# Linear attention and two feed-forward layers on one core: queries of blocks 1 to 8 loaded by halves of a head's components and turned by VectorE

## The chip, the cores and the metric

The kernel runs on one core of one Trainium2 chip. The metric is the device time of one execution in microseconds (us). The time before is 1531.42 us, the median of three runs (1531.21 to 1534.8).

## The reference, cut to what matters

```python
# q, k, v: [8, 8, 576, 64] (batch, head, sequence, component); all inputs float32 in the reference
kv  = einsum('bhsd,bhse->bhde', k, v)
out = einsum('bhsd,bhde->bhse', q, kv)
rms = sqrt(mean(out * out, axis=-1) + 1e-06)
x   = (out / rms * g_norm)              # to [4608 tokens, 512]
h   = x @ w_in1                         # 512 x 2048
x   = (max(h, 0) + alpha * min(h, 0)) @ w_out1
h   = x @ w_in2
out = (h * sigmoid(1.702 * h)) @ w_out2
```

The kernel reads the weights as 64-bit words and turns them into 32-bit values itself.

## The kernel before

The 4608 tokens are nine blocks (0 to 8) of 512 tokens. Layer 0 of block 0, 1 and 2 and layer 1 of block 0 run as plain products (`plain`): a step m is one 128-wide piece of the 2048 inner columns, made by `gemm_in` (12 matmuls of 128x512, bank h) and, two steps later, `gemm_out` (12 matmuls, bank y). All other blocks run two at a time through `pairs`, with seven products in place of eight (banks X, Z, V, W). Every value and weight is split into a high and a low part (`note_split`: ScalarE writes the high part, VectorE the rest), and a product is three matmuls; all of them are issued at L937.

The program has three stretches. The start reads keys, values and queries, and makes block 0's input. The plain stretch follows, in 48 steps: block 0 up to piece MH - 1, block 1 whole, the rest of block 0, block 2. The pairs and the last plain block take the remainder. Along the plain stretch the kernel also does the attention of blocks 1 to 8 (the jobs below), turns the sixteen weight pieces of layer 0 (`weight`, `weight1`), and begins their sums (`weights1`), which the pairs read back from memory.

A job is a piece of attention work put between two half-steps of the plain stretch; `JOBS` gives each block its first half-step and the number of half-steps over which its jobs are spread. Job k (`job_kv`) makes keys times values. Job q (`job_q`) prepares queries for two heads, p = 0 to 3 for the block's eight heads. Job o (`job_out`) multiplies queries by keys-times-values on TensorE (tile ops), and ScalarE and VectorE do the norm (L583 mean of squares, L599 scaling). Job x (`job_x`) hands the result on: for blocks 2 to 8 VectorE transposes 32x32 squares (L638) and SyncE stores it (L645).

Job q before: the block's queries are loaded by SyncE with tokens on the partitions (L523, runs of 64 components, 256 bytes). For each p, TensorE transposes four 128x128 squares into PSUM (L545, tile qTps), and ScalarE copies the bank to SBUF (L553, tile qT). For blocks 1 to 8 that is 128 transposes and 32 copies.

The order of the work is not written out by hand. Every operation is noted with its engine, its estimated cost and its dependences (`note`); `arrange` then plays these against one another and gives each operation a place in its engine's queue and a place in SBUF; `emit` writes the queues in that order. Each engine takes its queue strictly in order. All DMAs are issued from SyncE's queue. SBUF places are shared by many tiles, so a name such as dr__477 or kvb in a row is that of the place's first tenant, not of the value.

Of the kernel before, what the change touches and what calls it, by code (L numbers as in the profile page):

```python
# [10 lines left out]
F32 = mybir.dt.float32  # L11
# [8 lines left out]
P = 128  # L20
# [4 lines left out]
MH = 6  # L25
# [25 lines left out]
ACT2, DVE2, POOL2 = 1.06, 1.17, 2.35  # L51
KB1, B256, B512 = 1.1, 1.77, 1.3

HOP_ASIDE = 0.8
AHEAD = {"wt": 10.0, "xs": 20.0, "xc": 80.0, "gr": 8.0, "ld": 14.0, "raw": 45.0, "w2p": 12.0, "x": 15.0}
SLACK = 10.0
SPARE = {"8": 3, "4": 3, "2": 3}
SPARE_W = {"8": 1, "4": 2, "2": 3}

BACKLOG = 2.0  # L60
URGENT = 10.0
LD_LOW = {"4": 10}
ADDS = 4
PASSES = 12
SEED = 153
GAP, SLOW = 1.8, 3.4

RINGS = (3, 2, 2, 6)
# [11 lines left out]
def linear_attention_two_ffn_kernel(  # L80
# [52 lines left out]
    xd = {j: dram.tile([KC, P, TB], F32, name=f"xd{j}") for j in range(min(2, PLAIN), NB)}  # L133
# [23 lines left out]
    pe_clock = [0.0]  # L157

    def note(eng, cost, fn, reads=(), writes=(), new=(), ahead=None, slack=SLACK, low=None, mb=0.0, two=False, aside=False, calm=False):
# [6 lines left out]
        o.aside, o.calm = aside, calm  # L166
# [5 lines left out]
        for key in reads:  # L172
            if key in last_write:
                o.deps.add(last_write[key])
            readers.setdefault(key, []).append(o)
# [12 lines left out]
        ops.append(o)  # L188

# [22 lines left out]
    def arrange(before, ahead, urgent, spread):  # L212
# [6 lines left out]
        for o in ops:  # L219

            if o.eng == "PE":
                o.late = before[o.n] if before else o.clock
                now_ = o.late + o.cost
                o.base = o.late
            else:
                o.late = now_ + o.slack if o.slack is not None else 1e9
            o.land = o.cost + (LAND + o.mb / RATE if o.eng == "SP" else 0.0)
        for o in reversed(ops):
            late = [a.late - spread * (HOP if a.eng != o.eng else 0.0) - o.land for a in after[o.n]]
            o.late = min([o.late] + late)  # L230
        unit = [0.0] * (UNITS + 8)
# [69 lines left out]
        def arrive(o):  # L301
# [4 lines left out]
            if o.ahead is not None and line and o.late - ahead * o.ahead > line[0].late:  # L306
                held.append((o.late - ahead * o.ahead, o.n, o))
# [20 lines left out]
        def choose(e, spare, dma_at):  # L328
# [3 lines left out]
            for o in ready[e]:  # L332
# [7 lines left out]
                if o.need:  # L340
                    r = room_at(o, spare and o.late > t + urgent)
# [10 lines left out]
        for _ in range(len(ops)):  # L352
# [15 lines left out]
            if line and o is line[0]:  # L368
                line.popleft()
# [10 lines left out]
            if o.two or o.eng == "POOL":  # L380
                other = "POOL" if o.two else "DVE"
                cost += max(0.0, port[other] - t)
# [33 lines left out]
    def emit():  # L416
        found = (1e9, None)
        rng = random.Random(SEED)
        for i in range(PASSES):
            options = (1.0, URGENT, 1.0) if i < 2 else (rng.uniform(0.7, 1.3), rng.uniform(0.0, 30.0), rng.uniform(0.5, 4.0))  # L420
            got = arrange(found[1] if i else None, *options)
# [24 lines left out]

    def load_kv(b, p):
# [13 lines left out]

        note("SP", 2 * ISSUE, load, writes=[(key, 0)], new=[(key, [P, 2 * TB], F32, "4")], ahead=AHEAD["ld"], slack=None, mb=0.52 * KB1, low=LD_LOW if b > 1 else None)
        if p == 0:
            note("SP", 2 * ISSUE, load_rest, writes=[(("kR",), 0), (("vR",), 0)], ahead=AHEAD["ld"], slack=None, mb=0.26 * B256)

# [15 lines left out]
    def job_kv(b, p):  # L481
# [13 lines left out]

        for i in pp:
            load_kv(b, i)
# [11 lines left out]
    def job_q(j, p):  # L509

        bank, qT = ("qTps", j, p), ("qT", j, p)
        src = ("ldq", j, p if j == 0 else 0)

        def load0():
# [6 lines left out]
        def load(t):  # L521
            for off, n, b, s in runs((NT4 * j + t) * P, P):
                nc.sync.dma_start(  # L523
                    out=tl(src)[off : off + n, t * TB : (t + 1) * TB].rearrange("p (h d) -> p h d", h=H),
                    in_=q[b, :, s : s + n, :].rearrange("h p d -> p h d"),
                )

        if j == 0:
            note(
# [876 lines left out]
```

## Time and profile before

| | |
|---|---|
| median of three runs | 1531.42 us |
| profiled execution, whole time | 1531.49 us |
| profiled execution, span from first to last instruction | 1529.6 us |
| TensorE matmul, busy | 1504.7 us (98%), 7376 matmul instructions recorded |
| TensorE weight load, busy | 1244.8 us (81%) |
| VectorE, busy | 1119.4 us (73%) |
| ScalarE, busy | 760.4 us (50%) |
| GpSimd, busy | 329.8 us (22%) |
| hardware DMA queue, share of 16 engines | 78.9% |
| mean granted TensorE clock | 0.997 |

The whole time of the profiled execution is 1.9 us above its span. Shares are means over stretches that differ much, so the profile is to be read by stretch: first where TensorE stands idle, then what the removed instructions take from its stream, then how full VectorE and the DMA engines are where the added work goes.

### The profile page before, as it was taken

What the parts mean: (1) busy time and instruction counts of PE and PEld (TensorE: products, weight loads), DVE (VectorE), ACT (ScalarE), POOL (GpSimd) and SP (SyncE); (2) the same over time, 40 slices, a digit from 0 to 9 for tenths busy, and PEclk for the clock granted to TensorE, in tenths of its full rate; (3) what the DMA queues carried; (4) which work ended last, traced back from release to release, by engine and by line L of the source; (5) the groups of instructions that cost most, each with busy time, mean ns of one, the idle gap of its engine ahead of it and who ended that gap; (6) DMA issues with size and microseconds to landing.
All of it is one profiled execution on the core that took longest, in us unless ns stands there. A gap on an engine that the chain in (4) does not pass through costs nothing.

```text
span 1529.6 us, 19788 instructions
## 1 busy us (share of the span) xinstructions
PE 1504.7 (98%) x7376; PEld 1244.8 (81%) x7376; DVE 1119.4 (73%) x1148; ACT 760.4 (50%) x971; POOL 329.8 (22%) x282
## 2 busy tenths in 40 slices
PE   5999999999999999999999999999999999999998
PEld 4788888888788888888888888888888888888886
DVE  4899965698979998999899668654855485547511
ACT  4876544545555455554555555444634463444221
POOL 2444540685231134123424220000000000000000
PEclk9999999999999999999999999999999999999999
DMA  9998785858989799989998987676767676756962
GB/s 274 323 325 255 209 237 140 247 177 268 340 278 327 234 346 327 331 288 350 332 322 279 356 314 237 207 236 205 238 208 235 205 237 208 234 193 205 286 195 83
DMA packets 240495, 393.49 MB, mean 257 GB/s; under 512 B 93968, under 2 KB 124688, under 8 KB 240400
## 3 DMA queue, kind: packets, MB, share of 16 engines
q1 hardware_dynamic: 240400, 392.23, 78.9%
q8 instruction: 59, 0.97, 0.3%
q14 instruction: 36, 0.29, 0.1%
HBM read 302.00 MB, written 90.18 MB: 256 GB/s over the span
## 4 chain that ended last, share of the span: by engine, by line
PE 96%; DVE 1%; DMA 1%; ACT 1%; issue 1%; POOL 0%; SPq 0%; DVEq 0%; ACTq 0%; POOLq 0%
PE V L937 20%; PE X L937 19%; PE W L937 15%; PE Z L937 15%; PE y L937 11%; PE h L937 11%; PE ops L568 2%; PE kvps L477 1%; PE qTps L545 1%; DMA ldkv<-in_v_dram 1%; POOL ldkv L784 0%; SPq L453 0%; DVE gl L1184 0%; PE xTps L660 0%; POOL kvb L784 0%
## 5 line engine op out<-in xcount | busy, mean ns | idle before, releaser
L937 PE MATMUL V<-gr,pi 128*128 128x512 f32 x852 | 215.7, 389 | 0.5 <-DVE gr L706 0.5
L937 PE MATMUL X<-xc,gs 128*128 128x512 f32 x840 | 213.0, 389 | 0.1
L937 PEld LDWEIGHTS V<-gr,pi 128*128 128x128 f32 x852 | 159.8, 188 | 34.0 <-DVE gr L706 0.9
L937 PEld LDWEIGHTS X<-xc,gs 128*128 128x128 f32 x840 | 157.6, 188 | 33.2 <-DVE gl L1184 0.5
L937 PE MATMUL Z<-xc,gs 128*128 128x512 f32 x660 | 166.8, 389 | 0.0
L937 PE MATMUL W<-gr,pi 128*128 128x512 f32 x636 | 161.1, 389 | 0.0
L937 PEld LDWEIGHTS Z<-xc,gs 128*128 128x128 f32 x660 | 123.9, 188 | 25.7
L937 PE MATMUL h<-x,w 128*128 128x512 f32 x546 | 140.5, 398 | 3.5 <-DVE x L672 3.4
L937 PEld LDWEIGHTS W<-gr,pi 128*128 128x128 f32 x636 | 119.4, 188 | 24.8
L937 PE MATMUL X<-xc,pi 128*128 128x512 f32 x492 | 124.3, 389 | 0.0
L937 PE MATMUL V<-gr,gs 128*128 128x512 f32 x480 | 121.5, 389 | 0.0
L937 PEld LDWEIGHTS h<-x,w 128*128 128x128 f32 x546 | 101.3, 190 | 24.3 <-DVE x L672 4.0
L937 PE MATMUL y<-gs,w 128*128 128x512 f32 x480 | 118.8, 395 | 0.9 <-DVE gs L706 0.9
L706 DVE TENSOR_TENSOR gr<-gt,gr 128x1024 fp32r<-128x1024 f32 x84 | 103.6, 1239 | 17.8 <-ACT gr L699 17.7
L1182 DVE TENSOR_TENSOR gt<-Z,gt 128x512 f32<-128x512 f32 x64 | 44.0, 688 | 97.4 <-PE Z L937 92.8
L937 PEld LDWEIGHTS X<-xc,pi 128*128 128x128 f32 x492 | 92.3, 188 | 19.4 <-ACT gl L1192 0.3
L699 ACT ACTIVATE gr<-gt 128x1024 fp32r<-128x1024 f32 x84 | 87.9, 1054 | 36.2 <-DVE gt L901 14.3
L937 PEld LDWEIGHTS V<-gr,gs 128*128 128x128 f32 x480 | 90.1, 188 | 18.7
L937 PEld LDWEIGHTS y<-gs,w 128*128 128x128 f32 x480 | 88.3, 188 | 19.3 <-DVE gs L706 1.2
L706 DVE TENSOR_TENSOR gr<-gl,gr 128x1024 fp32r<-128x1024 f32 x56 | 73.3, 1309 | 31.9 <-ACT gr L699 31.9
L937 PE MATMUL W<-gr,gs 128*128 128x512 f32 x372 | 93.6, 389 | 0.0
L937 PE MATMUL Z<-xc,pi 128*128 128x512 f32 x348 | 88.0, 389 | 0.0
(515 smaller groups left out, 2554.5 us busy)
## 6 DMA issues: line engine op xcount, KB each, us to landing
gs<-w1wi SPq DMA_DIRECT2D x68, 512.0 KB, 4.8
pi<-w0wo SPq DMA_DIRECT2D x63, 512.0 KB, 5.0
pi<-w1wo SPq DMA_DIRECT2D x63, 512.0 KB, 3.7
gs<-w0wi SPq DMA_DIRECT2D x60, 512.0 KB, 5.5
pi<-w1wi SPq DMA_DIRECT2D x53, 512.0 KB, 4.7
gs<-w1wo SPq DMA_DIRECT2D x51, 512.0 KB, 3.7
raw<-in_moe_w_in_dram SPq DMA_DIRECT2D x16, 1024.0 KB, 7.6
raw<-in_moe_w_out_dram SPq DMA_DIRECT2D x16, 1024.0 KB, 7.8
```

The lines of the kernel that those rows point to most:

```text
L477: nc.tensor.matmul(tl(("kvps", b))[sl, p, sl], lhsT=lhsT, rhs=rhs, start=(r == 0), stop=(r == R), skip_group_check=True)
L545: nc.tensor.transpose(tl(bank)[:, t * P : (t + 1) * P], tl(src)[:, x : x + P], ident)
L568: nc.tensor.matmul((tl(("ops", j, heads[i])) if j else tl(bank)[:, i])[off : off + n, t], lhsT=tl(("qT", j, heads[i]))[:, t * P + off : t ...
L699: "ACT", ACT2 if both else ACT, lambda: nc.scalar.activation(out=part(0), in_=value(), func=AF.Copy, scale=1.0 if scale is None else scale),
L706: nc.vector.tensor_tensor(out=part(1), in0=value(), in1=high, op=ALU.subtract)
L937: nc.tensor.matmul(o, lhsT=x, rhs=y, start=start and n == 0, stop=stop and n == 2, skip_group_check=True)
L1182: nc.vector.tensor_tensor(out=val(), in0=tl(bank), in1=val(), op=ALU.add)
```

## The change

For blocks 1 to 8 the queries are loaded in another layout, so that 32x32 transposes alone turn them. One load (tile ldq) holds four heads (two values of p). Its partitions are four groups of 32: head h of a pair (0 or 1) and half a of its 64 components. Within a group lie 32 tokens on the partitions and 32 components in a run (128 bytes). VectorE's stream transpose of the whole 128x1024 tile swaps tokens and components within each 32x32 square, which gives qT for two p at once. TensorE's 128 transposes and ScalarE's 32 copies for these blocks are gone; block 0 keeps its own.

A load is issued per group of 32 partitions, and per p, or per run of 32 tokens where the block crosses from one batch entry into the next with fewer than 128 tokens. SyncE issues 240 such DMAs in the program where it issued 36 before; the piece of the most common form in block 1 is 32x14x32 (57 KB), the smallest 32x2x32 (8 KB).

The diff also changes the planner's numbers (`AHEAD`, `SPARE`, a table `SHIFT` of due times), and with them the order on every engine. MH goes from 6 to 8, so that block 0 runs eight pieces before block 1 starts. The jobs of blocks 3 to 8 are spread over later half-steps. In `weights1` one GpSimd addition of 128x1024 becomes four of 128x256, sixteen times. HALF = 8 and KEPT = 8 equal the number of pairs of pieces, so the branches on them are not taken, and no other work is added.

```diff
-MH = 6
+MH = 8
...
-J1 = (2, 8)
+J1 = (1, 9)
...
-JOBS = {2: (13, 11), 3: (24, 11), 4: (35, 11), 5: (46, 11), 6: (57, 11), 7: (68, 11), 8: (79, 11)}
+JOBS = {2: (12, 11), 3: (28, 10), 4: (39, 11), 5: (51, 12), 6: (71, 8), 7: (79, 9), 8: (88, 7)}
...
-RINGS = (3, 2, 2, 6)
+RINGS = (3, 1, 2, 7)
...
     def job_q(j, p):
+        if j:
+            return job_q_turned(j, p // 2) if p % 2 == 0 else None
...
+    def job_q_turned(j, pp):
+        src, qT = ("ldq", j, pp), ("qT", j, pp)
+        todo = []
+        for off, n, b, s in runs(TB * j, TB):
+            u = off // 32
+            if n // 32 < 4:
+                todo += [(u + x, None, b, s + 32 * x, n) for x in range(n // 32)]
+            else:
+                todo += [(u, p, b, s, n) for p in range(2)]
+        def load(i):
+            h, a = i // 2, i % 2 * 32
+            to = tl(src)[32 * i : 32 * (i + 1)].rearrange("x (p n f) -> x p n f", p=2, f=32)
+            for u, p, b, s, n in todo:
+                if p is None:
+                    nc.sync.dma_start(
+                        out=to[:, :, u],
+                        in_=q[b, 4 * pp : 4 * pp + 4, s : s + 32, a : a + 32].rearrange("(p h) x f -> h x p f", h=2)[h],
+                    )
+                else:
+                    nc.sync.dma_start(
+                        out=to[:, p, u : u + n // 32],
+                        in_=q[b, 4 * pp + 2 * p + h, s : s + n, a : a + 32].rearrange("(n x) f -> x n f", x=32),
+                    )
+        for i in range(4):
+            note(
+                "SP", 0.4 * len(todo), lambda i=i: load(i), reads=[(src, 0)] if i else [], writes=[(src, i)],
...
+        note(
+            "DVE", DVE2, lambda: nc.vector.transpose(tl(qT), tl(src)),
+            reads=[(src, i) for i in range(4)], writes=[(qT, 0), held_by[qT]],
+            new=[(qT, [P, 2 * TB], F32, "4")], low={"4": 2},
+        )
...
                 def whole(da=da, w=w):
                     t = tl(w).bitcast(F32).rearrange("p e h i f -> p (e h) i f")
-                    nc.gpsimd.tensor_tensor(
-                        out=tl(da).rearrange("p (n f) -> p n f", n=4), in0=t[:, :, 0], in1=t[:, :, 1], op=ALU.add
-                    )
+                    for n in range(4):
+                        nc.gpsimd.tensor_tensor(
+                            out=tl(da)[:, n * HB : (n + 1) * HB], in0=t[:, n, 0], in1=t[:, n, 1], op=ALU.add
+                        )
```

The queues below are those of the place where block 1's queries come in, while block 0's first pieces run. Line numbers of the changed kernel differ: matmuls stand at L1035 (L937 before), the attention product at L647 (L568), the weight conversion at L850, L852 and L865 (L761, L763 and L776), the low parts at L793 and L795 (L706 and L708), the first layer's activation at L999 (L901), the new loads at L606 and L611, and the stream transpose of queries at L624.

TensorE before, from the fourth piece of block 0 (h) to block 1's first attention products (ops):

```order
L937 MATMUL h<-x,w 128x512 x6
L545 MATMUL qTps<-ident,ldq 128x128 x8
L937 MATMUL h<-x,w 128x512 x3
L545 MATMUL qTps<-ident,ldq 128x128 x8
L937 MATMUL h<-x,w 128x512 x3
L937 MATMUL y<-gs,w 128x512 x3
L568 MATMUL ops<-kvb,da 64x128 x2
```

TensorE in the changed kernel, from the fourth piece (h) to the same products:

```order
L1035 MATMUL h<-x,w 128x512 x12
L1035 MATMUL y<-gs,w 128x512 x12
L1035 MATMUL h<-x,w 128x512 x12
L647 MATMUL ops<-kvb,dr__487 64x128 x2
```

The sixteen transposes are gone, and the products of block 1 stand 21 matmuls of 512 columns later in the stream than before.

VectorE in the changed kernel, at that place (gs is the low part that y's matmuls read, w a weight's low part, xn a weight in conversion):

```order
L793 TENSOR_TENSOR gs<-ldkv,gs 128x512
L850 TENSOR_SCALAR xn<-xn 128x1024
L852 TENSOR_SCALAR xn<-xn 128x1024
L624 STREAM_TRANSPOSE dr__487<-kvb 128x1024
L793 TENSOR_TENSOR w<-dr__487,w 128x4x256
L624 STREAM_TRANSPOSE dr__487<-ldkv 128x1024
L865 SCALAR_TENSOR_TENSOR xn<-raw,xn 128x512 x2
L999 SCALAR_TENSOR_TENSOR ldkv<-ldkv,alpha_sb 128x512
```

Two stream transposes have come into VectorE's queue; a weight's low part stands between them, and a weight conversion and the next activation behind them.

SyncE's queue before, where block 1's queries are loaded (raw is a weight piece of 1 MB):

```order
L460 DMA kR<-in_k_dram 64x8x64
L460 DMA kR<-in_v_dram 64x8x64
L523 DMA ldq<-in_q_dram 64x8x64 x2
L728 DMA raw<-in_moe_w_in_dram 128x4x256
L733 DMA raw<-in_moe_w_out_dram 128x2x512 x2
L523 DMA ldq<-in_q_dram 128x8x64 x3
L728 DMA raw<-in_moe_w_in_dram 128x4x256
```

SyncE's queue in the changed kernel, from the sixth weight piece on (eight of the 32 query pieces stand earlier, before and behind the third weight piece):

```order
L817 DMA raw<-in_moe_w_in_dram 128x4x256
L822 DMA raw<-in_moe_w_out_dram 128x2x512 x2
L606 DMA kvb<-in_q_dram 32x2x32 x2
L611 DMA kvb<-in_q_dram 32x14x32 x2
L606 DMA kvb<-in_q_dram 32x2x32 x2
L611 DMA kvb<-in_q_dram 32x14x32 x2
L606 DMA kvb<-in_q_dram 32x2x32 x2
L611 DMA kvb<-in_q_dram 32x14x32 x2
L606 DMA ldkv<-in_q_dram 32x2x32 x2
```

Twenty-four small query pieces now stand behind the eighth weight piece, where five larger ones stood between the third and the seventh.

## Rows read from the trace of the kernel before

**Rows 1.** Windows: stretch, busy per engine, granted clock, DMA share, GB/s.

```profile
core 0: us, PE busy (x) PEld busy (x) DVE busy (x) ACT busy (x) POOL busy (x), PEclk, DMA share, GB/s
0.00:62.00 62.00, 43.91 (x347) 34.71 (x348) 39.24 (x54) 38.17 (x57) 21.92 (x30) 0.94 1.03 289
62.00:210.00 148.00, 148.00 (x1020) 123.91 (x1020) 133.13 (x161) 96.94 (x139) 69.63 (x62) 1.00 0.85 259
210.00:375.00 165.00, 164.23 (x951) 136.41 (x950) 122.65 (x137) 80.70 (x119) 74.71 (x57) 1.00 0.72 213
375.00:1437.00 1062.00, 1061.48 (x4681) 878.02 (x4680) 809.30 (x777) 523.61 (x622) 163.49 (x135) 1.00 0.80 269
1437.00:1530.00 93.00, 87.04 (x385) 71.73 (x383) 15.05 (x22) 20.97 (x36) 0.00 (x0) 0.99 0.53 170
```

**Rows 2.** TensorE's waits: line, who released it, us in total, times, longest.

```profile
PE kvps L477 <- DMA kvb<-in_v_dram: 4.4, 1, 4.4
PE h L937 <- DVE x L672: 3.4, 1, 3.4
PE ops L568 <- ACT kvb L553: 2.3, 1, 2.3
PE xTps L660 <- DVE xn L599: 1.9, 1, 1.9
```

**Rows 3.** TensorE's timeline: start, us, line, form, count, idle before.

```profile
52.05 0.94 PE L937 MATMUL h<-x,w 128*128 128x512 f32 x3
52.83 1.04 PE L545 MATMUL qTps<-ident,ldq 128*128 128x128 f32 x8
53.62 0.94 PE L937 MATMUL h<-x,w 128*128 128x512 f32 x3
54.40 0.84 PE L937 MATMUL y<-gs,w 128*128 128x512 f32 x3
55.74 1.30 PE L568 MATMUL ops<-kvb,da 128*64 128x128 f32 x10 [0.49 <-ACT da L553]
...
83.54 2.88 PE L937 MATMUL h<-x,w 128*128 128x512 f32 x12
86.26 0.60 PE L545 MATMUL qTps<-ident,ldq 128*128 128x128 f32 x4
86.62 3.00 PE L937 MATMUL y<-gs,w 128*128 128x512 f32 x12
89.45 0.60 PE L545 MATMUL qTps<-ident,ldq 128*128 128x128 f32 x4
```

**Rows 4.** Instructions of the query job: count, duration ns least, median, most.

```profile
L545 PE MATMUL qTps<-ident,ldq x128: 270/272/273, 51.3 to 329.2; 128*128 128x128 f32 x128
L553 ACT COPY ldkv<-qTps x9: 570/585/592, 10.7 to 245.5; 128x512 f32<-128x512 f32 x9
```

**Rows 5.** Nearest operations on VectorE and GpSimd, same columns.

```profile
L638 DVE STREAM_TRANSPOSE qT<-qT x2: 1235/1240/1245, 266.3 to 275.2; 128x1024 f32<-128x1024 f32 x2
L889 POOL TENSOR_TENSOR dr__477<-w x5: 2382/2780/2854, 186.9 to 301.2; 128x1024 f32<-128x1024 f32 x5
```

**Rows 6.** Windows while query loads (L523) fill the DMA engines.

```profile
286.00:287.00 1.00, 1.00 (x6) 0.80 (x6) 0.70 (x1) 0.36 (x1) 1.00 (x2) 1.00 1.02 393
289.00:290.00 1.00, 1.00 (x6) 0.84 (x5) 1.00 (x2) 0.00 (x0) 0.96 (x1) 1.00 1.31 217
290.00:291.00 1.00, 1.00 (x6) 0.84 (x5) 1.00 (x1) 0.21 (x1) 0.92 (x2) 1.00 1.27 195
```

**Rows 7.** DMA issues: count, KB each, median us to landing.

```profile
ldq<-in_q_dram SPq DMA_DIRECT2D x28, 256.0 KB, 5.4
xd<-qT SPq DMA_DIRECT2D x12, 128.0 KB, 3.7
```

**Rows 8.** SyncE's issue durations at L1282: ns least, median, most.

```profile
L1282 SPq DMA_DIRECT2D out_dram<-kvb x44: 337/490/1153, 985.0 to 1436.7; - x44
```

**Rows 9.** SyncE's timeline at block 1's queries: start, us, line, count.

```profile
33.97 10.74 SPq L523 DMA_DIRECT2D ldq<-in_q_dram  x3
```

More of the change, by code (lines that the diff above doesn't have):

```diff
@@ L188, in note, with ahead_of, spare_of @@
         ops.append(o)
+    def ahead_of(what):
+        return (AHEAD_START if pe_clock[0] < START_T else AHEAD if pe_clock[0] < EARLY_T else AHEAD_LATER)[what]
+    def spare_of(now, later):
+        return now if pe_clock[0] < EARLY_T else later
     opened = {}
@@ L210, in tl, with arrange @@
         return tiles[key]
-    def arrange(before, ahead, urgent, spread):
+    def arrange(before, first, later, shift, stop=None):
         after = [[] for _ in ops]
@@ L221, in arrange @@
             if o.eng == "PE":
-                o.late = before[o.n] if before else o.clock
+                o.early = o.clock < EARLY_T
+                o.late = before[o.n] if before and not o.early else o.clock + LEAD
                 now_ = o.late + o.cost
@@ L226, in arrange @@
                 o.late = now_ + o.slack if o.slack is not None else 1e9
+                o.early = now_ < EARLY_T + LEAD
             o.land = o.cost + (LAND + o.mb / RATE if o.eng == "SP" else 0.0)
         for o in reversed(ops):
-            late = [a.late - spread * (HOP if a.eng != o.eng else 0.0) - o.land for a in after[o.n]]
+            o.way = START_WAY if o.early and o.clock < START_T else first if o.early else later
+            late = [a.late - o.way[2] * (HOP if a.eng != o.eng else 0.0) - o.land for a in after[o.n]]
             o.late = min([o.late] + late)
+        for o in ops:
+            if o.eng != "PE":
+                o.late += shift.get(o.group, 0.0)
         unit = [0.0] * (UNITS + 8)
@@ L305, in arrive @@
             o.ready = t
-            if o.ahead is not None and line and o.late - ahead * o.ahead > line[0].late:
-                held.append((o.late - ahead * o.ahead, o.n, o))
+            if o.ahead is not None and line and o.late - o.way[0] * o.ahead > line[0].late:
+                held.append((o.late - o.way[0] * o.ahead, o.n, o))
                 held.sort()
@@ L340, in choose @@
                 if o.need:
-                    r = room_at(o, spare and o.late > t + urgent)
+                    r = room_at(o, spare and o.late > t + o.way[1])
                     if r is None:
@@ L368, in arrange @@
             if line and o is line[0]:
+                if stop is not None and o.clock >= stop:
+                    return t, start, fin, place
                 line.popleft()
@@ L381, in arrange @@
                 other = "POOL" if o.two else "DVE"
-                cost += max(0.0, port[other] - t)
+                cost += min(0.65 if o.two else 9.0, max(0.0, port[other] - t))
                 port[o.eng] = t + cost
@@ L563, in job_out @@
         batches = sorted({b for _, _, _, b, _ in parts})
+        if any(made.get(b % 2) != b for b in batches):
+            raise ValueError("keys and values of another batch")
         def fn(hs):
@@ L880, in weights1 @@
     def weights1():
-        for k in range(NQ):
+        for k in (*range(HALF, NQ), *range(HALF)):
             for kind in ("wi", "wo"):
+                group[0] = ("s", 0, kind, k)
+                if k >= KEPT:
+                    sums(0, kind, k, ("da", 0, kind, k))
+                    continue
                 da, w = ("da", 0, kind, k, "again"), ("w", 0, kind, k)
@@ L1049, in gemm_out @@
                 )
+            if open_:
+                continue
             if m == M - 1:
```

228 lines of the change are left out of this document (138 added, 90 removed), and 12 rows, old and new, of the table SHIFT.

## The prediction

> **What bounds the kernel now.** I read the windows first [rows 1]. TensorE is busy all 148 us from 62 to 210, 164.2 of 165 us from there to 375, and 1061.5 of 1062 us in the pairs. From 62 us to the end of the pairs it stands idle 0.8 + 0.5 = 1.3 us. So the kernel is bound by the length of TensorE's own stream, apart from the start, where it is busy 43.9 of 62 us, and the tail of some 6 us. In the start the idle time has many owners: first data, first weights, norm, block 0's input [rows 2]. The granted clock is at its upper level (1.00) from 62 us on and averages 0.94 in the start, where the idle times lie [rows 1].
>
> What hides behind TensorE has room, but unevenly. VectorE is busy 133.1 of 148 us (90%) from 62 to 210, and 122.7 of 165 us (74%) to 375. The DMA engines are at 1.03 in the start, 0.85 and then 0.72 [rows 1]. The queries of blocks 1 to 8 all come in within these stretches: the transposes run from 51.3 to 329.2 us [rows 4].
>
> **TensorE's transposes (removed).** Their price must be read as pace, not as duration. One lasts 272 ns [rows 4], but the next instruction starts before it ends. A group of four that stands between a piece's twelve matmuls and the next twelve: the twelve alone go from 83.54 to 86.26, 2.72 us; four transposes and twelve matmuls go from 86.26 to 89.45, 3.19 us [rows 3]. The difference is 0.47 us, which holds the change of form on both sides too. A group of eight with three matmuls goes from 52.83 to 54.40, 1.57 us; three matmuls at 2.72/12 = 0.227 us are 0.68, so eight transposes cost 0.89 us [rows 3]. In the timeline the 128 transposes stand in 24 groups of four and 4 of eight, from the first to the last in [rows 4]: 24 x 0.47 + 4 x 0.89 = 11.3 + 3.6 = 14.9 us. TensorE is busy around them, and nothing in the change puts another instruction into its stream. All 14.9 us therefore leave the path, as long as what feeds TensorE keeps up.
>
> The Trainium skill (TensorE: Matmul & The Clock Gate, Part 4: PE-mode transpose) gives about 275 ns for one 128x128 transpose in a kernel's context; as a duration this trace agrees with 272 ns, but as a price it would make 128 x 0.275 = 35.2 us, and the starts in the rows speak against that.
>
> **ScalarE's copies (removed).** 32 x 0.585 us = 18.7 us less on an engine that is half busy [rows 1, 4]. It counts nothing by itself, but activations can start earlier.
>
> **VectorE's transposes (added).** A stream transpose of 128x1024 took 1.24 us in the jobs of the normalised result [rows 5]. Sixteen make 19.8 us. They lie beside TensorE's work. The sum over the first 375 us is 39.2 + 133.1 + 122.7 = 295.0 us of work before and 314.8 after [rows 1]. The order spreads it: blocks 3 to 8 get their jobs later, where VectorE had 42 us free. From 62 to 210 it had 14.9 us free; with three to four blocks in that time (2.5 us each) there would still be 5 to 7 us. So I cost them at nothing, covered by 90% to 95% full VectorE; if the cover fails the next thing late is gs, the low part that y's matmuls read.
>
> **GpSimd.** Sixteen additions of 2.8 us become 64 smaller ones [rows 5]. GpSimd is busy 166 of the first 375 us [rows 1]; nothing on TensorE's path waits for these sums soon. Bound: no loss, and at best some VectorE time, since it waits less long where both want the same port. I take zero.
>
> **Loads.** SyncE issues 204 DMAs more. A 128 KB store took 0.49 us to issue [rows 8], so 204 x 0.49 = 100 us, some 12 us per block, spread over more than 300 us. Behind them in the queue stand weights and keys. On the DMA engines: with query loads of 256-byte runs alone the rate was 195 to 217 GB/s at full share, against 393 just before [rows 6]. A block's 1.05 MB took about 5.1 us at that. No row has 128-byte runs. One bound is no loss (the time goes by bytes), the other is half the rate (it goes by runs): 10.2 us, 5.1 us more per block, 41 us for eight. I take the upper one, since the rate already halved once with the run. From 62 to 375 the engines have 0.15 x 148 + 0.28 x 165 = 68 us free [rows 1], so it is covered on average. It is not covered in the start, where the share is 1.03. There the order puts 24 of block 1's 32 pieces behind the eighth weight piece.
>
> The Trainium skill (DMA: Bandwidth & Descriptors, Bandwidth) says that transfers under 64 KB are ruled by their descriptors, and (Specifications) that under 512 bytes per run the full rate isn't reached; the rate of the 256-byte loads agrees with the second, and no run here shows the first, which speaks against pieces of 8 and 57 KB. By it the third rival below would come true.
>
> **The start.** Its order is new: the fourth piece, y of the second and the fifth piece now all come before block 1's products. Against before that is 21 matmuls more (4.8 us) and 16 transposes less (1.8 us) ahead of them, so they fall due about 3 us later, at 58.7 us in place of 55.74 [rows 3]. The data come later as well: before, the last three of block 1's five loads began at 33.97 and kept SyncE 10.7 us [rows 9], until 44.7; now 24 pieces begin about there, at 0.49 us each 12 us: until 57, with a landing of 3.7 us for small transfers [rows 7] and a transpose of 1.24 us still to come, 62 us. Against this, SyncE can issue ahead while the eight pieces queued earlier are already in. So a wait between 0 and 3.3 us is to be expected at these products, and I take 1.5. MH = 8 needs the eight weight pieces of the first four pairs sooner, but they now stand ahead of the queries. Block 0's own input may win or lose 2 us by the new order (the waits of 3.4 and 1.9 us [rows 2]); I take zero.
>
> **The sum.** Profiled execution 1531.5 - 14.9 + 1.5 = 1518.1 us. Its time stands at the median of the three runs (1531.4), so 1518.0 is also the forecast for the median. The last blocks and the tail keep their work, and there I count nothing.
>
> **The rivals.**
> 1. *The forecast*: TensorE's stream is shorter by 14.9 us, the start gives back 0 to 3.3: 1516.5 to 1520, with 2 us either way for block 0's input 1514.5 to 1522.
> 2. *The start gains too*: the new order removes most of the waits for block 0's input and the attention ahead of it, 3.4 + 1.9 + 2.3 us [rows 2]. For it speaks that VectorE now scales the first result before it converts a weight; against it, that block 0's later queries are read ahead of the first weight. 1531.5 - 14.9 - 7.6 = 1509.
> 3. *Late queries stop VectorE*: VectorE takes its queue in order. A stream transpose that waits for its pieces holds the weight's low part, the next conversion and the next activation behind it, and these hold TensorE. If each of the sixteen transposes stands at the head of the queue for one landing of 3.7 us [rows 7], and half of it reaches TensorE, that is 16 x 1.9 = 30 us: 1531.5 - 14.9 + 30 = 1547, slower. It decides from 14.9/16 = 0.93 us per transpose on. Against it: the DMA engines have 68 us free after 62 us [rows 1], so pieces can be in well before. For it: VectorE is 90% full where this happens, and can't catch up fast.
> 4. *Only the start loses*: block 1's first two transposes come one block's extra load time late, 5.1 us, with the 3.3 us above: 8.4 us, 1531.5 - 14.9 + 8.4 = 1525.
> 5. *Transposes cost their duration*: 128 x 0.272 = 34.8 us off [rows 4]: 1497. The starts in [rows 3] leave next to nothing for it.
>
> **How the numbers follow.** Forecast 0.58, start gains 0.14, late queries 0.07, only the start loses 0.18, full duration 0.03. A measurement can tell about 0.3%, 4.6 us: the borders are 1526.8 and 1536.0. Rival 4 reaches over 1526.8 in about a third of its cases. So faster is 0.58 + 0.14 + 0.12 + 0.03 = 0.87, same 0.06, slower 0.07. For the range I leave out the full duration, late queries and the far third of rival 4, and the lower part of rival 2: 1510 to 1526. It holds both ends of the loads' cost as far as they fall in the start.
>
> **What would show it.** The query transposes' group on TensorE has 16 instructions left, block 0's. TensorE's busy time falls by about 15 us and that of VectorE rises by about 20; TensorE stays busy all of the time from 65 us to the pairs. The wait list shows TensorE's products (ops) behind VectorE for at most 3 us, once, between 55 and 65 us. The prediction is wrong if TensorE's idle time between 62 and 375 us rises by more than some 5 us, with y or h released by VectorE's low parts and, before these, VectorE idle at the stream transpose until a DMA: that is rival 3. If TensorE's busy time falls by much less than 15 us at the same clock, the price of the transposes is wrong.

## The result and the profile after

The changed kernel took 1540.78 us (median; 1539.69 to 1543.64) beside 1532.09 us for the kernel before on the same chip: 1.0057 times as long, 95% interval 1.0047 to 1.0067. It is slower by some 8.7 us, where 13.4 us less had been predicted.

The first view to read is again the windows, of the changed kernel; the columns are those of [rows 1].

```profile
0.00:62.00 62.00, 40.68 (x308) 33.12 (x308) 39.01 (x53) 33.76 (x49) 24.05 (x30) 0.92 0.88 244
62.00:210.00 148.00, 137.66 (x871) 112.53 (x872) 132.25 (x158) 89.47 (x121) 77.77 (x76) 0.99 0.82 245
210.00:375.00 165.00, 158.86 (x960) 131.61 (x959) 117.21 (x149) 74.19 (x109) 86.59 (x97) 0.98 0.84 246
375.00:1437.00 1062.00, 1060.61 (x4678) 877.70 (x4677) 813.71 (x778) 530.18 (x622) 158.25 (x128) 1.00 0.79 268
```

Between 62 and 375 us TensorE now stands idle 10.3 + 6.1 = 16.5 us; before it was 0.8 [rows 1]. The start lost 3.2 us more. The pairs are nearly untouched. The DMA engines are at 0.82 and 0.84, with room left, and VectorE did no more work between 62 and 375 us than before (117.2 + 132.3 = 249.5 us against 255.8): neither of the two resources that the prediction weighed ran out. What did run out shows in three more views. First TensorE's waits in the changed kernel (line, who released it, us, times, longest):

```profile
PE kvps L526 <- DMA ldkv<-in_v_dram: 9.4, 3, 7.8
PE xTps L739 <- DVE xn L678: 8.0, 2, 7.4
PE ops L647 <- DVE sq L624: 3.9, 1, 3.9
PE y L1035 <- DVE gs L793: 3.2, 2, 1.9
PE ops L647 <- DVE qT L624: 2.2, 1, 2.2
PE h L1035 <- DVE w L795: 1.7, 1, 1.7
PE ops L647 <- DVE dr__487 L624: 1.4, 1, 1.4
```

Three waits of the attention products (ops) end at the stream transpose of queries (L624). Its own view lists what VectorE sat idle for ahead of it: in us, and times.

```profile
L624 DVE STREAM_TRANSPOSE qT<-sq x2: 1234/1240/1247, 292.5 to 339.4; 128x1024 f32<-128x1024 f32 x2
...
  DMA g<-in_q_dram: 10.7, 2
  DMA dr__1188<-in_q_dram: 5.3, 2
```

The transposes cost 1.24 us, as taken. But VectorE stood still at them until query pieces had landed: 16.0 us in these two rows. And here is why the pieces were late, in SyncE's timeline (start, us, line, count):

```profile
280.30 3.72 SPq L611 DMA_DIRECT2D g<-in_q_dram  x4
284.06 7.10 SPq L611 DMA_DIRECT2D sq<-in_q_dram  x12
291.25 0.38 SPq L822 DMA_DIRECT2D raw<-in_moe_w_out_dram  x1
291.68 8.10 SPq L611 DMA_DIRECT2D g<-in_q_dram  x12
```

Twenty-eight query pieces kept SyncE's queue for 18.9 of 19.5 us: 0.6 to 0.9 us each. For most of that time the DMA engines had little to do (windows of 2 us; the last two columns are their share and the GB/s):

```profile
282.00:284.00 2.00, 2.00 (x10) 1.65 (x10) 0.57 (x1) 0.69 (x1) 0.00 (x0) 1.00 1.05 403
...
286.00:288.00 2.00, 2.00 (x66) 1.93 (x62) 0.09 (x1) 1.49 (x2) 0.00 (x0) 1.00 0.34 53
288.00:290.00 2.00, 2.00 (x10) 1.62 (x10) 1.96 (x4) 0.00 (x0) 0.00 (x0) 1.00 0.26 41
290.00:292.00 2.00, 2.00 (x10) 1.66 (x9) 1.59 (x3) 0.69 (x1) 1.89 (x2) 1.00 0.41 66
```

From a full share at 403 GB/s the rate falls to 41 to 66 while the pieces are issued one by one. Compare [rows 6]: the old loads of 256 KB kept the engines full. So the bound in this stretch is SyncE's queue. Its issues, added up from the rows of its timeline, fill 134.9 of 148 us (62 to 210) and 128.8 of 165; before it was 74.7 and 73.0. A row reaches from its first issue to the end of its last, so the short pauses between its issues are in these sums. Some pauses have a cause of their own: SyncE's DMAs take eight semaphores in turn, and in the traces of before, of the changed kernel and of all runs that issue from SyncE alone no issue starts before the DMA eight places ahead of it has landed. In the changed kernel 36 pauses between 62 and 375 us, 22.8 us together, end within 0.2 us of such a landing. Pieces thus hold the queue by the time that their issues take and by their landings.

### The profile page after: what moved, and what is told of

It reads as the page before. It is cut to its first block, busy times and chain, and to the rows that moved or that the text cites. A ratio compares the mean times of both kernels' runs of the same rounds, so it can differ in the third digit from the quotient of the medians.

```text
span 1540.1 us, 19832 instructions
## 1 busy us (share of the span) xinstructions
PE 1496.4 (97%) x7248; PEld 1236.2 (80%) x7248; DVE 1124.6 (73%) x1164; ACT 751.0 (49%) x939; POOL 346.7 (23%) x330
## 4 chain that ended last, share of the span: by engine, by line
PE 81%; DMA 8%; SPq 5%; DVE 4%; issue 1%; POOL 1%; ACT 0%; DVEq 0%; ACTq 0%; POOLq 0%
PE X L1035 19%; PE V L1035 19%; PE Z L1035 15%; PE W L1035 15%; PE y L1035 6%; PE h L1035 6%; SPq L611 2%; DMA raw<-in_moe_w_out_dram 2%; DMA ldkv<-in_v_dram 2%; DMA raw<-in_moe_w_in_dram 1%; PE ops L647 1%; DMA g<-in_q_dram 1%; SPq L502 1%; SPq L606 1%; DMA w1wo<-wsp 1%
## 5 line engine op out<-in xcount | busy, mean ns | idle before, releaser
L1035 PE MATMUL V<-gr,pi 128*128 128x512 f32 x1284 | 325.1, 389 | 0.0
L1035 PE MATMUL X<-xc,pi 128*128 128x512 f32 x1284 | 325.0, 389 | 0.0
L1035 PEld LDWEIGHTS V<-gr,pi 128*128 128x128 f32 x1284 | 241.0, 188 | 50.0
L1035 PEld LDWEIGHTS X<-xc,pi 128*128 128x128 f32 x1284 | 241.0, 188 | 50.0
L1035 PE MATMUL Z<-xc,pi 128*128 128x512 f32 x996 | 251.7, 389 | 0.1
L1035 PE MATMUL W<-gr,pi 128*128 128x512 f32 x924 | 233.9, 389 | 0.0
L1035 PEld LDWEIGHTS Z<-xc,pi 128*128 128x128 f32 x996 | 186.9, 188 | 39.3 <-DVE gt L1286 0.5
L1035 PEld LDWEIGHTS W<-gr,pi 128*128 128x128 f32 x924 | 173.5, 188 | 36.0
L1035 PE MATMUL h<-x,w 128*128 128x512 f32 x540 | 135.0, 396 | 1.7 <-DVE w L795 1.7
L1035 PE MATMUL y<-gs,w 128*128 128x512 f32 x504 | 124.5, 394 | 3.9 <-DVE gs L793 3.2
L1035 PEld LDWEIGHTS h<-x,w 128*128 128x128 f32 x540 | 101.7, 190 | 23.6 <-DVE w L795 2.1
L793 DVE TENSOR_TENSOR gr<-gl,gr 128x1024 fp32r<-128x1024 f32 x56 | 71.8, 1281 | 58.1 <-ACT gr L786 58.1
L1035 PEld LDWEIGHTS y<-gs,w 128*128 128x128 f32 x504 | 94.2, 189 | 24.5 <-DVE gs L793 4.0
L793 DVE TENSOR_TENSOR gr<-gt,gr 128x1024 fp32r<-128x1024 f32 x84 | 104.8, 1255 | 4.2 <-ACT gr L786 4.2
L786 ACT ACTIVATE gr<-gl 128x1024 fp32r<-128x1024 f32 x56 | 59.3, 1059 | 36.0 <-PE V L1035 20.9
L793 DVE TENSOR_TENSOR gr<-t,gr 128x1024 fp32r<-128x1024 f32 x40 | 50.0, 1249 | 33.3 <-ACT gr L786 33.2
L960 POOL TENSOR_TENSOR qT<-qT 128x256 f32<-128x256 f32 x48 | 57.5, 1199 | 54.9 <-DVE wsp L793 45.5
```

What stands on the lines that cost most here:

```text
L786: "ACT", ACT2 if both else ACT, lambda: nc.scalar.activation(out=part(0), in_=value(), func=AF.Copy, scale=1.0 if scale is None else scale),
L793: nc.vector.tensor_tensor(out=part(1), in0=value(), in1=high, op=ALU.subtract)
L960: lambda o=o, a=a, b=b, op=op: nc.gpsimd.tensor_tensor(out=quarter(o), in0=quarter(a), in1=quarter(b), op=op),
L1035: nc.tensor.matmul(o, lhsT=x, rhs=y, start=start and n == 0, stop=stop and n == 2, skip_group_check=True)
```

## The experiments

All theories below speak of the same loss: if the transposes gave their 14.9 us, some 24 us came back elsewhere (14.9 + 8.7 = 23.6). The candidates: the number of issues (theory 1), the 128-byte runs (2), VectorE's added work (3), the planner's new order (4).

**The same order with 64 loads, and the same pieces with longer runs.** Both keep the changed kernel's order on the computing engines, and change only the load function; the queries that they read are not the reference's.

```diff
 a_long: a load (32 partitions) is one DMA of 128 KB
+            nc.sync.dma_start(out=tl(src)[32 * i : 32 * (i + 1)],
+                in_=flat[z : z + 32 * 1024].rearrange("(x w) -> x w", x=32))
 b_runs: the 240 pieces stay, each from one contiguous place
-                        in_=q[b, 4 * pp + 2 * p + h, s : s + n, a : a + 32].rearrange("(n x) f -> x n f", x=32),
+                        in_=flat[z : z + 32 * w].rearrange("(x n f) -> x n f", x=32, f=32),
```

> The changed kernel with its order on TensorE, VectorE, ScalarE and GpSimd kept row for row; only the query loads of blocks 1 to 8 are other: 64 DMAs of 128 KB in 4 KB runs from a contiguous place in place of 240 small ones with 128-byte runs (so queries are not the ones of the reference). Theory 1, SyncE's queue is filled by the number of small pieces: TensorE's idle time from 62 to 375 us falls from 15.7 us to under 6, and the time from 1540.8 to about 1526. Theory 2, the 128-byte runs slow the DMA engines: the same, about 1526. Theory 3, the sixteen stream transposes overfill VectorE: no change, 1540 within 3. Theory 4, all is the new order of the start: no change within 3 either, and the idle time of 21 us before 62 us stays.

> The same 240 DMAs with the same sizes, targets and places in the queue, but read from contiguous places, so that runs are 128 bytes only in the 32 smallest ones and 512 bytes to 2 KB in the others (queries are again not the reference's). Theory 1, the number of issues decides: 1540 within 4, TensorE idle from 62 to 375 us still over 11 us. Theory 2, the 128-byte runs decide: like the 64 long DMAs, about 1526. Theories 3 and 4: 1540 within 3.

Measured: 1525.42 us with 64 long loads (0.9955 of before, 0.9941 to 0.9968), and 1541.27 us with 240 pieces of longer runs (1.0058, 1.0038 to 1.0077). So 15.4 of the changed kernel's 1540.8 us go with the number of issues (fewer pieces are also larger ones, since the bytes stay), and nothing goes with the run length while the number stays. The windows of both, first 64 loads, then longer runs:

```profile
62.00:210.00 148.00, 142.66 (x900) 117.85 (x901) 140.70 (x168) 93.92 (x128) 86.13 (x84) 0.99 0.81 250
210.00:375.00 165.00, 165.00 (x1002) 137.39 (x1001) 127.02 (x156) 77.95 (x111) 84.15 (x90) 1.00 0.81 256
```

```profile
62.00:210.00 148.00, 136.98 (x873) 112.61 (x872) 133.12 (x159) 90.49 (x122) 77.99 (x76) 0.99 0.77 246
210.00:375.00 165.00, 158.25 (x962) 131.19 (x961) 115.02 (x146) 73.19 (x108) 86.52 (x97) 0.99 0.79 244
```

With 64 loads TensorE is idle 5.3 us in these two windows, with 240 pieces 17.8. VectorE carries the same transposes in both, and with 64 loads it even gets more done: theory 3 falls.

**One half of the diff at a time.** c_path is the kernel before with its planner's numbers and only the new query path; d_order has the new numbers with the old path.

```diff
 c_path, against before
-    def job_q(j, p):          # loads by tokens, TensorE transposes, ScalarE copies
+    def job_q(j, p):          # block 0 so; blocks 1 to 8: job_q_turned(j, p // 2)
 d_order, against the changed kernel
-            return job_q_turned(j, p // 2) if p % 2 == 0 else None
+            # job_q of the kernel before, whole
```

> The kernel before with the new query path alone (loads by halves, stream transposes), and the planner's numbers of before. Theories 1 and 2: TensorE loses the 14.9 us of transposes and waits more after 62 us, 1522 to 1535, idle after 62 us over 5 us. Theory 3: the same, but with VectorE never idle at a stream transpose. Theory 4, the new order of the start is to blame: idle in the first 62 us about 18 us as before, and 1517 within 3.

> The changed kernel with the query path of before (256-byte loads, transposes on TensorE, copies on ScalarE) and the planner's new numbers. Theory 4: the loss of the start of about 7 us stays, 1537 within 3. Theories 1 and 2: the waits after 62 us go (under 4 us) and only what the start loses stays, 1531 to 1538. Theory 3: as theories 1 and 2. If it comes to 1531 or less, the new numbers cost nothing by themselves.

Measured: c_path 1543.69 us (1.0065, 1.004 to 1.009), d_order 1538.59 us (1.0038, 1.0025 to 1.0051). Each half alone is slower. c_path lies over what any theory gave; d_order is where theory 4 put it, and it waits 3.0 us from 62 to 375 us, as theories 1 and 2 had it. d_order's windows:

```profile
0.00:62.00 62.00, 40.94 (x313) 33.45 (x313) 38.79 (x53) 34.01 (x49) 23.62 (x30) 0.92 0.99 268
62.00:210.00 148.00, 145.61 (x946) 120.32 (x947) 120.42 (x150) 97.93 (x140) 67.25 (x68) 1.00 0.85 251
375.00:1437.00 1062.00, 1059.64 (x4672) 876.29 (x4671) 815.96 (x779) 528.79 (x622) 157.79 (x128) 1.00 0.81 269
```

Against [rows 1], TensorE loses 3.0 us in the start, 2.4 from 62 to 210 and 1.8 in the pairs: the new order costs something by itself, 5.9 us by the medians and 7.4 by the spans of the profiled executions. In the start of the changed kernel the first wait for keys and values is 7.8 us in place of 4.4 [rows 2], and TensorE waits 7.4 us for the second half of block 0's input. Before, it had products of the first layer (h) to do meanwhile; now the first weight's low part is made at 33.62 us (L795) in place of 27.26 (L708), so there are none.

**Old order, long loads; then 128 of them.** c_long joins c_path with a_long's loads; c_128 cuts each load in two. The order is c_path's row for row.

```diff
 c_128, against c_long
-                in_=flat[z : z + 32 * 1024].rearrange("(x w) -> x w", x=32),
+            for y in range(2):   # out: columns TB * y to TB * (y + 1)
+                    in_=flat[z : z + 32 * 1024].rearrange("(y x w) -> y x w", y=2, x=32)[y],
```

> The kernel before, its planner's numbers unchanged, with the new query path, but with 64 query loads of 128 KB (from the wrong places: what is multiplied is not the reference's queries) in place of the 240 pieces. Against the run of the new path with the old numbers (1543.7 us) only the number of issues differs. Theory 1 (the count of issues on SyncE): the forecast's own sum, 1531.5 - 14.9 = 1517, and up to 3 us for first transposes: 1516 to 1521. Theory 2 (VectorE's added transposes can't be hidden without a new order): 1526 to 1535, with TensorE waiting for low parts (gs, w) from 62 us on.

> The run with 64 long loads under the old planner's numbers, each load cut into two of 64 KB: 128 DMAs in place of 64 or 240, the order on every engine row for row the same, bytes the same (again from the wrong places). Theory 1a (the queue costs only when nearly full; 64 more issues at 0.5 us make SyncE some 85 to 95 busy of 148 and of 165 us): 1519 to 1523. Theory 1b (each issue costs the same, 24.6 us for the 176 between 64 and 240): 1519.1 + 64 x 0.14 = 1528.

Measured: 1519.14 us (0.9909, 0.9894 to 0.9923) and 1518.77 us (0.9908, 0.989 to 0.9926). The prediction's own sum, 1518.0, is about what the new query path gives under the old planner's numbers when SyncE's queue has room. Windows of c_path (240 pieces), c_128 and c_long from 62 to 210 us:

```profile
62.00:210.00 148.00, 140.97 (x942) 116.54 (x942) 131.01 (x163) 88.71 (x122) 63.33 (x59) 0.97 0.85 235
```

```profile
62.00:210.00 148.00, 146.97 (x997) 122.22 (x996) 139.86 (x169) 92.93 (x129) 69.02 (x63) 1.00 0.81 252
```

```profile
62.00:210.00 148.00, 146.99 (x1002) 122.33 (x999) 139.85 (x170) 92.82 (x129) 67.57 (x63) 1.00 0.81 251
```

From 210 to 375 us TensorE is busy all 165 us in both of the latter, and 155.9 in c_path. The cost of an issue is thus no constant: theory 1a holds, 1b doesn't. From 64 issues to 128 nothing is lost, from 128 to 240 24.9 us. In that last step the runs shrink too, to 128 bytes, which c_long's expectation passed over. That this costs nothing is shown in the changed kernel's order only, by b_runs, which also gives the price of the count by itself there, 1541.3 - 1525.4 = 15.9 us. SyncE's issues fill 70.2 and 77.1 us of the two stretches with 64 loads, 86.2 and 92.4 with 128, 132.5 and 133.7 with 240: the queue costs once it is nearly full.

The form of the cost is a convoy, seen best in c_path. VectorE's timeline, then TensorE's:

```profile
128.46 1.22 DVE L928 SCALAR_TENSOR_TENSOR ldkv<-ldkv,alpha_sb 128x512 f32<-128x512 f32 x1
133.72 1.25 DVE L574 STREAM_TRANSPOSE da<-ldkv 128x1024 f32<-128x1024 f32 x1 [4.04 <-DMA ldkv<-in_q_dram]
134.88 0.65 DVE L733 TENSOR_TENSOR gs<-ldkv,gs 128x512 fp32r<-128x512 f32 x1
```

```profile
129.91 1.52 PE L964 MATMUL h<-x,w 128*128 128x512 f32 x6
135.11 2.12 PE L595 MATMUL ops<-kvb,da 128*128 128x128 f32 x8 [3.68 <-DVE da L574]
```

VectorE waits 4.04 us for the last piece, and TensorE 3.68 us for VectorE. Such a wait can cost twice. In the changed kernel the twenty products after the wait of 3.88 us at 327.52 took 4.45 us; with 64 long loads the twenty at 150.57, behind a wait of 2.08 us, took 2.70. The windows of the two groups differ in the granted clock, 0.50 (the lower of its two levels) against 1.00:

```profile
327.52:331.97 4.45, 4.45 (x21) 3.34 (x21) 0.71 (x1) 0.59 (x1) 4.08 (x6) 0.50 0.90 293
150.57:153.27 2.70, 2.70 (x21) 2.12 (x22) 2.03 (x3) 2.70 (x4) 0.00 (x0) 1.00 0.56 211
```

Time lost in this way counts as busy, so TensorE's idle time alone understates the loss.

**Other queues.** e_act (the changed kernel) and c_act (c_path) issue the pieces from ScalarE, e_pool from GpSimd.

```diff
-                    nc.sync.dma_start(
+                    nc.scalar.dma_start(      # e_act, c_act; nc.gpsimd.dma_start in e_pool
```

> The changed kernel with one edit: its 240 query pieces are issued from ScalarE's queue, not SyncE's; pieces, sizes, runs and the order on every other engine stay. Theory 1 (the pieces cost because each holds SyncE's queue for about half a microsecond, with keys, weights and later queries behind it): about the time of the run with 64 long loads, 1525 us, 1522 to 1531 with some loss on ScalarE, which has to issue for some 100 us more and was half busy; TensorE's wait of 3.9 us for the stream transpose at 327 us goes. Theory 2 (so many small transfers are slow in the DMA engines, whoever issues them): 1538 to 1543, as the changed kernel. Theory 3 (a piece at the head of ScalarE's queue that waits for its buffer holds the activations): over 1545, with TensorE waiting on ScalarE.

> The changed kernel with its 240 query pieces issued from GpSimd's queue in place of SyncE's, nothing else. Theory 1 (SyncE's queue): about 1525, 1522 to 1531, if GpSimd issues a piece in about the time that SyncE does; it is busy 166 of the first 375 us, so 100 us more fit. Theory 2 (small transfers are slow in the DMA engines): 1538 to 1543. Theory 3 (GpSimd prices an issue higher than SyncE, or its issue holds VectorE): over 1543, with TensorE waiting on VectorE or on GpSimd's sums.

> The kernel before, its planner's numbers unchanged, with the new query path whose 240 pieces are issued from ScalarE's queue. Theory 1 (SyncE's queue): as the run with long loads, 1517 to 1523. Theory 2 (small transfers slow in themselves): 1538 to 1545. Theory 3 (pieces hold ScalarE's activations): over 1531, with TensorE waiting on ScalarE.

Measured: 1592.39 us (1.0379, 1.0362 to 1.0397), 1694.99 us (1.1053, 1.1035 to 1.1071) and 1578.69 us (1.0295, 1.0278 to 1.0312). Theory 3 of those lists fits by the time. Theory 1's numbers for these were wrong: in an order that the planner still makes for SyncE, a freed SyncE is no gain if the queue that takes over computes. TensorE's longest waits in e_act and e_pool name VectorE more than ScalarE or GpSimd, so the delay reaches it there mostly by way of VectorE; in c_act they name ScalarE (9.6 and 9.0 us). Because the new queue brings its own loss, these three runs don't tell theory 1 from theory 2 (small transfers are slow whoever issues them). Against theory 2 stand c_128, which loses nothing with pieces of 64 KB, and the low share of the engines while pieces are issued; no run isolates it. ScalarE issues a piece in a median of some 0.46 us as SyncE does, and its activations stand behind (timeline of e_act; ACTq is ScalarE's sequencer):

```profile
31.71 1.25 ACTq L606 DMA_DIRECT2D kvb<-in_q_dram  x2
33.00 1.03 ACTq L611 DMA_DIRECT2D kvb<-in_q_dram  x2
34.08 1.12 ACT L845 ACTIVATE ldq<-raw 128x1024 int32<-128x1024 uint32 x1 [5.31 <-DMA kvb<-in_q_dram]
```

On GpSimd a piece took longer, and its queue too holds sums and conversions:

```profile
L611 POOL DMA_DIRECT2D sq<-in_q_dram x48: 548/611/658, 314.0 to 500.9; - x48
```

The last pieces of queries were issued at 500.9 us there; with SyncE it was 350.1.

**Fewer pieces with the real queries.** c_fine is c_path with the planner told 0.5 us per piece, in a note of its own; in c_path one note stands for four to eight pieces, which are then issued in a bunch. c_half turns only blocks 2, 4, 6 and 8 (112 pieces). h_fine does both.

```diff
 c_fine
-                "SP", 0.4 * len(todo), lambda i=i: load(i), ...
+                    "SP", 0.5, lambda i=i, m=m: load(i, m), ...
 c_half
+TURNED = (2, 4, 6, 8)
```

> The kernel before with the new path for all of blocks 1 to 8, 240 pieces, where the planner is told 0.5 us for each piece in a note of its own (0.4 before, four to eight pieces in one note). Theory 1a (the sum of issues fills SyncE's queue, whatever their order): 1537 to 1545, TensorE again waiting for transposed queries (ops). Theory 1c (only the bunching was wrong, since the planner reckoned a piece too cheap): 1519 to 1528.

> The kernel before with its planner's numbers, where only blocks 2, 4, 6 and 8 take the new query path: 112 pieces in place of 240. TensorE's stream should be shorter by half of 14.9, 7.5 us. Theory 1a (SyncE's queue costs only once it is nearly full, as it was for 133 of 148 and 134 of 165 us with 240 pieces): the loss nearly goes, 1524 to 1527. Theory 1b (every piece costs the same on the path, so many as stood behind 24.6 us with 240 pieces against 64 long loads): half the gain against half the loss, 1533 to 1537.

> Both edits: blocks 2, 4, 6 and 8 alone on the new path, with 0.5 us for each piece in a note of its own. By theory 1a as the half alone, 1524 to 1527; by 1b 1533 to 1537; by 1c the lower end, 1524.

Measured: c_fine 1535.8 us (1.002, 1.0009 to 1.003), c_half 1529.12 us (0.9976, 0.9966 to 0.9985), h_fine 1528.64 us (0.9974, 0.9965 to 0.9984). c_fine lies between its two theories, and c_half and h_fine between 1a and 1b, nearer to 1a. Of c_path's loss against c_long, 24.6 us, a third (7.9) was bunching, and two thirds stay without it. Half of the blocks gives a kernel that beats both, by 3.4 us against before; its windows show why:

```profile
62.00:210.00 148.00, 147.52 (x1014) 122.71 (x1013) 130.16 (x163) 94.98 (x133) 69.56 (x61) 1.00 0.94 271
210.00:375.00 165.00, 165.00 (x937) 137.51 (x936) 132.40 (x143) 79.84 (x115) 81.02 (x64) 1.00 0.74 220
```

TensorE waits 0.5 us in all, as little as before the change, though SyncE's issues fill 120.1 us of the first stretch (92.5 of the second): full to 81% can still be hidden. It need not be: c_path's second stretch is as full, 133.7 of 165 us, and loses 9.1. The profiled execution (span 1524.5 us) is 5.1 us shorter than before's, but it is the fastest of its ten; the medians differ by 3.4, under half of the 7.5 us that half of the transposes are worth. Where the rest goes was not followed.

**A cut by batch entry.** c_batch loads a head's 576 tokens of one entry at a time, so that no block's end cuts a load: 128 pieces with the real queries. c_batch_long reads pieces of the same sizes from contiguous places in the same order (again not the reference's queries). c_late leaves block 1 on the old path.

```diff
 c_batch
+                    nc.sync.dma_start(out=to[g : g + 32],
+                        in_=q[b, 2 * p + h, s0:S, 32 * a : 32 * a + 32].rearrange("(n x) f -> x n f", x=32))
 c_late
+        if j == 2:
+            job_q_batch(1, p, S - P, "rest")
+        if j > 1:
+            return job_q_batch(j, p, 0, ("b", j)) if j < 8 else None
```

> The kernel before with its planner's numbers and all queries of blocks 1 to 8 turned by VectorE, but cut by batch entry in place of by block: a load brings one head's 576 tokens and half of its components, 32x18x32 (74 KB), 112 times, and 16 smaller ones for the last 64 tokens of the first entry: 128 pieces with the real 128-byte runs, 32 stream transposes of up to 576 columns in place of 16 of 1024. Theory 1a (the count of issues is what cost; 128 are well below what fills SyncE's queue): near the run of 128 pieces with long runs, 1518 to 1525, with a few us for queries that keep their place in SBUF longer. Theory 2 (runs of 128 bytes have a price of their own that the long-run controls did not have): 1528 to 1538, with the DMA share above that of the control from 62 to 375 us and TensorE waiting for transposed queries.

> The run cut by batch entry (128 pieces, 1540.6 us), order the same row for row and sizes the same, but each piece read from one contiguous place (runs of 2304 bytes in place of 128; the queries are then not the reference's). Theory 2 (the 128-byte runs cost, because the DMA engines are slower with them and SyncE's issues wait for those eight before): 1521 to 1528, with TensorE's idle time of 12.2 us between 62 and 210 us mostly gone and the pieces at 30 to 51 us issued in half the time. Theory 5 (the planner's order for this cut starves block 1, whatever the runs: 40 pieces stand ahead of the weights between 30 and 58 us): 1535 to 1541.

> The run cut by batch entry with block 1 left on the old path (TensorE's transposes), so that the 112 new pieces begin behind the start: 13 of the 14.9 us are to be gained. Theory 1a and 5 (count of issues, and the start's crowd in the cut by entry): 1519 to 1525. Theory 2 (128-byte runs cost wherever they stand): 1528 to 1537.

Measured: c_batch 1540.63 us (1.0042, 1.0024 to 1.006), c_batch_long 1535.43 us (1.0011, 1.0002 to 1.0021), c_late 1557.01 us (1.0151, 1.0134 to 1.0169). c_batch and c_late lie outside what any theory gave, c_batch_long where theory 5 put it. The runs of 128 bytes do cost here, 5.2 us by the medians, where the queue is filled to 110.2 of 148 us in the first stretch (95.8 with long runs); the rest stays with long runs and 128 issues, so it belongs to the order that the planner makes of this cut. In the profiled executions the 5.2 us are hardly idle time (12.2 us against 10.7 from 62 to 210); the granted clock of that stretch is 0.93 against 0.97. How the runs bring that about was not followed. c_batch's windows:

```profile
62.00:210.00 148.00, 135.81 (x829) 112.52 (x830) 121.75 (x162) 85.83 (x116) 46.80 (x48) 0.93 0.93 260
210.00:375.00 165.00, 164.16 (x996) 136.08 (x994) 130.29 (x153) 73.22 (x106) 72.57 (x53) 1.00 0.69 203
```

From 210 us on it loses next to nothing; from 62 to 210 it loses 12.2. Of these, TensorE's timeline gives 3.94 us to a weight's low part that is late at 65.48 us, with sixteen pieces issued from 30 to 41 us and sixteen more from 43 to 58, and three weight pieces between. But taking block 1's pieces out of the start did not help: c_late waits there for other things, 5.32 us for the remainder of keys and values and up to 2.8 us at a time for low parts, and SyncE's issues fill 124.0 of the 148 us. A batch's queries also hold their place in SBUF through two blocks; whether it is that which makes keys and weights late was not tried. So it stays open whether all blocks can be turned for 1519 us with the real queries.

## Why the prediction was wrong, point by point

*TensorE's transposes.* Right. With the queue free and the old order (c_long), TensorE's busy time falls from 1504.7 to 1490.6 us, 14.1 against the predicted 14.9, and the time from 1532.4 to 1519.1. Pace, not duration, was the price; the fifth rival is out.

*VectorE's transposes and the cover.* Right: 1.24 us each, and hidden as long as the data is there. c_long has VectorE at 139.85 of 148 us, and TensorE loses 1.0 us. *ScalarE's copies* and *GpSimd*: no wait of TensorE of over 1 us names them.

*Loads.* This is the step that failed. The prediction had worked out SyncE's added issue time, 204 x 0.49 = 100 us, a little low: the two stretches after 62 us hold 116 us more of it. Then it wrote "spread over more than 300 us" and turned to the DMA engines, where it found room. But a queue that issues in order has its own capacity, 148 and 165 us, of which 74.7 and 73.0 were taken; the sum should have been made there. With the 0.49 us of the stores it gives 74.7 + 73.0 + 100 = 248 of 313 us, 79%, which by the runs above is not yet a clear warning. But 0.49 us was a median from another stretch, and [rows 9] shows three loads that kept SyncE 10.7 us. In the two stretches themselves 217 issues filled 147.7 us, 0.68 each; with this mean the sum is 147.7 + 204 x 0.68 = 286 us, about 91%: nearly full, with keys and weights in the same line. Measured were 263.7 us, 84%, and 91% in the first stretch. The engines' share, on which the step rested, fell from 0.85 to 0.82 and rose from 0.72 to 0.84. The upper bound taken for the runs, 41 us of engine time, was sized on a resource that did not decide.

The rule of the Trainium skill (DMA: Bandwidth & Descriptors, Bandwidth), that transfers under 64 KB are ruled by descriptors, had been quoted against the pieces with "By it the third rival below would come true." The third rival came; the cause, as far as these runs show it, is another. With longer runs at the same count and sizes, and so fewer of them, nothing was gained (b_runs), and the engines stood at 0.26 to 0.41 while such pieces were issued. The same page (Issuing engines are not separate DMA queues) says that the sequencer time to initiate a DMA is "usually small relative to the DMA itself". For one piece that holds, 0.45 us against 2.5 to its landing; for 240 on one queue the trace disagrees.

*The start.* Mis-sized. The products of block 1 did wait, 1.4 us at 63.2 us, where 1.5 had been taken. But block 0's own input, taken as zero with 2 us either way, lost: the order alone costs 3.0 us by 62 us. Some 4 us more go later (d_order), and for that the sum had no term. Together the new order costs 6 to 7 us in place of 0. No row of before could size it, but the order could have warned: it puts the first weight's conversion behind the scaling of the first result, which the second rival counted as a gain.

*The sum, made again.* The profiled spans chain up: before 1529.6; with the new path and a free queue 1517.8 (-11.8); with the new order as well 1524.7 (+6.9); with 240 pieces 1540.1 (+15.4).

*The rivals.* The third (late queries stop VectorE, 1547) names the mechanism: VectorE idle at L624 until a DMA, and y and h behind its low parts. Its chance was 0.07, for the reason that the engines have 68 us free, the same wrong resource. Its price was about twice what was measured: the rival took 1.9 us on TensorE for each of the sixteen transposes, and TensorE's idle time rose by 15.7 us, 1.0 each, of which 2.2 us are the new order's (d_order), so that the 0.93 us from which it decides is just about reached. The 1540.8 us hold the start's loss as well; that the time came near the rival's 1547 is in part luck. The signs named in the prediction held: idle time from 62 to 375 us rose by 15.7 us, far over 5.

## What to carry to other kernels

A queue that issues DMAs is an engine with a capacity of its own: count the issues, multiply by the mean (not the median) time that an issue holds the queue in that stretch, add what the queue issues already, and compare with the stretch, before bytes and engine shares are looked at. Up to 58% filled nothing was lost here (c_128), at 81% nothing in one run (c_half) and 9.1 us in another (c_path), and at 90% 7.0 us: the share warns, but it doesn't decide alone. Where a change halves the pieces or is made for half of the blocks, part of the gain may be had without the loss. Moving the issues to an engine that computes was worse than leaving them here, in orders not made for it.

## What the runs showed of the hardware

Issuing a piece of 8 to 64 KB took a median of about 0.45 us on SyncE and ScalarE and 0.6 us on GpSimd; on SyncE single issues took from 0.31 to 5.7 us, and what made the long ones long is open. While SyncE issued such pieces alone (286 to 292 us), the DMA engines ran at a share of 0.26 to 0.41 and 41 to 66 GB/s. Runs of 128 bytes in place of 2304 cost 5.2 us over 128 pieces where the queue had room (c_batch), and runs of 128 bytes in place of mostly 512 to 2048 nothing that can be measured over 240 where it was full (b_runs). A transpose of 128x128 that lasts 272 ns took 14.1 / 128 = 0.11 us of TensorE's busy time in a full stream. After an idle time of 3.88 us TensorE's next products ran at a granted clock of 0.50; after one of 2.08 us they ran at 1.00.
